# Decode through two attention and MLP layers: four loads of the key and value cache, whose ends are cut off and loaded in three pieces over 64, 63 and 1 or 64, 51 and 13 partitions

## The chip, the core and the metric

The kernel runs on one core of a Trainium2 chip. The metric is the device time of one execution in microseconds. Before the change it is 1355.34 us, the median of three runs (1352.47 to 1356.29). A difference of about 0.3% (4 us) is what three such runs can tell from no change.

## The reference

One token passes through attention and an MLP, and both once more with the same weights and the same cache:

```python
x = x + _A_ref(_layernorm(x, axis=-1), A_k_cache, A_v_cache, A_wq, A_wo)
x = x + _B_ref(_layernorm(x, axis=-1), B_w1, B_w2)
x = x + _A_ref(_layernorm(x, axis=-1), A_k_cache, A_v_cache, A_wq, A_wo)
x = x + _B_ref(_layernorm(x, axis=-1), B_w1, B_w2)
```

`_A_ref` makes a query of 128 numbers for each of 32 heads, scores it against 8192 cached keys, takes the softmax, and sums 8192 cached values by it; `wo` brings the 32 x 128 sums back to the 640 numbers of x. `_B_ref` is a product with w1 (640 x 1728), a ReLU, and a product with w2. Everything is float32. Keys and values of one head are 8 MB, those of all heads 256 MB, and each layer needs all of them: the cache is what is moved.

## The kernel before

The cache and part of w2 come through one buffer in SBUF, `ring`, 128 partitions wide and some 149 KB deep in each. The host has laid the cache out so that a load is a rectangle: each of the 128 partitions takes one contiguous run. A head has four pieces of keys (`K_ALL`) and four of values (`V_ALL`), each 8 KB per partition, 1 MB over all 128. `UNITS` says which pieces are loaded together. Heads 2 to 26 (`FULL`) are one unit of eight pieces, 64 KB per partition.

The list `todo` holds the loads in the order in which they will be issued (lines 119 to 155): layer 0 with the heads upwards, layer 1 with the heads downwards, since the last heads of layer 0 are partly kept. For the `FULL` heads, `turning` (lines 124 to 132) walks round the first 18 slots of 8 KB, and cuts a head in two where it passes the end. So head 9 of layer 0 is one load into slots 0 to 7, head 15 of layer 0 is a load of six pieces into slots 12 to 17 and one of two into slots 0 and 1; in layer 1, head 15 is one load into slots 8 to 15 and head 9 one into slots 2 to 9.

`pump` (lines 190 to 208) issues loads from `todo` as long as their place in the ring is free. All go through SP's queue, at line 204. `scores` (keys, line 448) and `values` (line 497) are the matmuls that read a piece; each ends with `release`, which frees the place and calls `pump`. Tile works out the waits: a load waits for the matmuls that read what it overwrites, and a matmul for the loads that wrote what it reads. A load that completes counts up one of eight semaphores, `DMAHW0` to `DMAHW7`, which SP's and ACT's loads use in turn; before a load takes one, its issuer waits until the load that had it eight issues ago is complete, unless a wait before has shown that already.

ACT's queue carries the weights: `wq` and `wo` by groups of four heads (`load_wq`, `load_wo`), w1 once, the rest of w2 once. Scores and values of a head alternate on PE with the softmax on ACT and DVE (`exponentials`, lines 461 to 482), and with side work for the projections. At the end of each layer stands the MLP, whose product with w2 is at line 419.

Of the kernel before, what the change touches and what calls it, by code (L numbers as in the profile page):

```python
# [18 lines left out]
SK = 8192  # L19
# [41 lines left out]
UNITS[31] = HALVES[:2] + LAST  # L61
DROPPED = {30: 2}
KEPT = 3800
MIX_AT = [12, 16, 20, 24]
AHEAD = 3

# [5 lines left out]
def kind_of(unit, t):  # L72

    return unit[0] if unit[0] != "kv" else "k" if t < len(K_ALL) else "v"


def wide(kind, piece):

    if kind == "w":
        return D // 8  # L80
    return 4 * piece[2] * (1 if kind == "k" else DH) // 8


def size(unit):
    return sum(wide(kind_of(unit, t), piece) for t, piece in enumerate(unit[1]))
# [9 lines left out]
W2_ALL = [("w2", i) for i in range(len(W2_RUNS))]  # L95
RING = KEPT + 4 * F_TILES * D // 8


@with_exitstack
def decode_kernel(ctx: ExitStack, tc: tile.TileContext, x, kv, wq, wo, w1, w2, w2_rest, out):  # L100
    nc = tc.nc
# [12 lines left out]
    ring = consts.tile([P, 8 * RING], F32, name="ring")  # L114
    order = [(h, i) for h in range(H) for i in range(len(UNITS[h]))]
    kept = [u for u in order if u[0] >= min(DROPPED) and u[1] >= DROPPED.get(u[0], 0)]
    assert sum(size(UNITS[h][i]) for h, i in kept) == KEPT
    beside = [(1, u) for u in order if u[0] == 30 and u not in kept]
# [37 lines left out]
    source = {}  # L156
    for us, dram in ((order, kv), (W2_ALL, w2)):
        o = 0
        for u in us:
            n = 8 * P * size(UNITS[u[0]][u[1]])  # L160
# [5 lines left out]
    def place(layer, u, n):  # L166

        step = 512 if n % 512 == 0 else 8
        if layer:
            low, high = 0, RING  # L170
        elif u[0] in range(FULL[0]):
            low, high = 0, 16 * SLOT
        elif u[0] == "w2":
            low, high = KEPT, RING
        else:
            low, high = (3072, KEPT) if n == KEPT - 3072 else (0, 3072)
        at, best = low, None
        for a, m in sorted(live.values()) + [(high, 0)]:
            a = min(a, high)
            for base in (0, KEPT):  # L180
                c = base + -(-max(at - base, 0) // step) * step
                if a - c >= n and (best is None or a - at < best[1]):
                    best = c, a - at
            at = max(at, a + m)
        return None if best is None else best[0]

    def is_free(at, n):
        return all(a >= at + n or a + m <= at for a, m in live.values())

    def pump():  # L190
        while todo:
            layer, u, first, last, at = todo[0]
            unit = UNITS[u[0]][u[1]]
            ns = [wide(kind_of(unit, t), piece) for t, piece in enumerate(unit[1])]
            n = sum(ns[first:last])
            if at is None:
                at = place(layer, u, n)
                if at is None:
                    return
            elif not is_free(at, n):  # L200
                return
            todo.pop(0)
            o = 8 * sum(ns[:first])
            nc.sync.dma_start(ring[:, 8 * at : 8 * (at + n)], source[u][:, o : o + 8 * n])
            for t in range(first, last):
                live[layer, u, t] = at, ns[t]
                at_of[layer, u, t] = ring, 8 * at
                at += ns[t]
# [13 lines left out]
    def release(L, u, t):  # L222
        if (L or u not in kept) and at_of[key(L, u, t)][0] is ring:
            del live[key(L, u, t)]
            pump()
# [22 lines left out]
    nc.sync.dma_start(xr, x)  # L248
    load_wq(0, nc.sync)
    pump()  # L250
    load_wo(0, nc.sync)

# [305 lines left out]
    def mixing():  # L558

        wc = mix[:, :D]  # L560
        s = work.tile([P, 1], F32, name="m_s")
        nc.vector.tensor_reduce(s, wc, AX.X, ALU.add)
        nc.vector.scalar_tensor_tensor(
            wc, s.to_broadcast([P, D]), -1.0 / D, wc, op0=ALU.mult, op1=ALU.add
        )
        yield "pe"
        pt = ps_m.tile([P, 512], F32, name="px")
        for c in range(4):
            nc.tensor.transpose(pt[:, c * P : (c + 1) * P], wc[:, c * DR : c * DR + P], ident)
        yield "dve"  # L570
        nc.scalar.copy(wct[:, :4].rearrange("p c d -> p (c d)"), pt)
        yield "pe"
        pt = ps_m.tile([P, 512], F32, name="px")
        for g in range(4):
            nc.tensor.matmul(
                pt[32 * g : 32 * g + 32, :P],
                wc[:, g * DR + P : (g + 1) * DR],
                ident,
                start=True,
                stop=True,  # L580
            )
        yield "dve"
        nc.scalar.copy(wct[:, 4], pt[:, :P])  # L583

    def mixing_quarter(g):

        pt = ps_m.tile([P, 512], F32, name="px")
        f, n = F_AT[g], F_ROWS[g]
        for c in range(NB):
            nc.tensor.matmul(  # L590
                pt[:, :n],
                wct[:, c],
                w1_t[:, c, f : f + n],
                start=(c == 0),
                stop=(c == NB - 1),
            )
            yield "pe" if c < NB - 1 else "dve"
        nc.scalar.copy(mix[:, f : f + n], pt[:, :n])
# [13 lines left out]
    def attention_and_mlp(L, xr, s):  # L612
# [68 lines left out]
        def due(h):  # L681
# [17 lines left out]
            if where == 11:  # L699
                slow.append([mixing(), "dve"])  # L700
            if where in MIX_AT:
                slow.append([mixing_quarter(MIX_AT.index(where)), "pe"])

# [264 lines left out]
```

## Time and profile before

| | before |
|---|---|
| median of 3 runs | 1355.34 us |
| the profiled execution, its own time | 1351.49 us |
| its span, first to last instruction | 1349.7 us |
| granted clock of TensorE, mean | 0.809 |
| busy: PE, PE's weight loads, DVE, ACT | 799.3, 270.4, 251.4, 59.2 us |
| bytes moved, mean pace | 575.17 MB, 426 GB/s |
| PE before line 448 (scores), idle for loads of the ring | 329.6 us |

The profile is of one execution, made by the hardware. Engines are PE (matmuls), PEld (its weight loads), DVE, ACT, POOL and SP; a q behind a name means the sequencer that waits and issues for it. L204 is line 204 of the kernel before. A DMA is issued by SP or ACT and carried out by 16 DMA engines that all loads share; the profile counts the packets that they moved, by queue (q1 is SP's, q10 ACT's, q8 and q14 fetch instructions), and the share of time in which the 16 were busy, but it doesn't name the engine of a packet. The busy time by window lists, for a stretch of time in us: its length, busy time and count of PE, PEld, DVE, ACT and POOL, the granted clock, the mean busy share of the 16 DMA engines, and GB/s. Shares a little over 1 come from packets that overlap. The chain lists what ended last at each step, in order of time: start, length, and the work.

### The profile page before, as it was taken

To read this page: it belongs to the slowest core of one execution; us is meant where nothing else is said; L and a number is where in the kernel's file an instruction comes from. 1 tells how busy PE (TensorE), PEld (TensorE's weight loads), DVE (VectorE), ACT (ScalarE), POOL (GpSimd) and SP (SyncE) were. 2 spreads that over 40 slices of the span, in tenths; PEclk is the share of its full clock that TensorE was granted. 3 is DMA by queue.
4 is the path that set the end of the run, shared out by engine and by line. 5 is a ranking of instruction groups with operands and counts; after the bars stand their busy time and mean duration, and the time that the engine had idled before them with its cause. 6 is when DMAs were issued, how large, how long until landed. Compare 5 with 4: busy or idle time off the path is not lost.

```text
span 1349.7 us, 13544 instructions
## 1 busy us (share of the span) xinstructions
PE 799.3 (59%) x6048; PEld 270.4 (20%) x6048; DVE 251.4 (19%) x794; ACT 59.2 (4%) x149; POOL 2.9 (0%) x10
## 2 busy tenths in 40 slices
PE   5455555554654655457787754555566554656658
PEld 2011111211211211122242211111121121212214
DVE  1111111221211211122122211122111211111212
ACT  0000000000000000000000000000000000000000
POOL 0000000000000000000000000000000000000000
PEclk8777677878978976788799777797778778777879
DMA  9999999999999999999999999999999999999997
GB/s 392 445 419 437 432 428 441 417 431 436 439 426 432 430 435 422 448 417 420 425 405 423 435 431 432 432 431 436 438 434 424 421 435 443 429 420 438 429 418 322
DMA packets 24977, 575.17 MB, mean 426 GB/s; under 512 B 2772, under 2 KB 2904, under 8 KB 5336
## 3 DMA queue, kind: packets, MB, share of 16 engines
q1 hardware_dynamic: 20312, 531.89, 91.8%
q10 hardware_dynamic: 4608, 42.44, 7.5%
q8 instruction: 47, 0.77, 0.2%
q14 instruction: 10, 0.08, 0.0%
HBM read 574.31 MB, written 0.00 MB: 426 GB/s over the span
## 4 chain that ended last, share of the span: by engine, by line
DMA 65%; PE 27%; DVE 5%; issue 1%; ACT 1%; ACTq 0%; SPq 0%; DVEq 0%
DMA ring<-in_kv 64%; PE ps L448 13%; PE outs L497 8%; DVE h_t L459 2%; PE px L387 1%; DVE pt L477 1%; PE pm L464 1%; ACT p L473 1%; DMA wo_t<-in_wo 1%; DVE p L516 1%; PE acc L419 1%; PE px L419 1%; PE acc L603 0%; PE px L590 0%; DVE pT L479 0%
## 5 line engine op out<-in xcount | busy, mean ns | idle before, releaser
L448 PE MATMUL ps<-ring,spread_q 128*32 128x512 f32 (+2 forms) x2072 | 331.0, 787 | 334.5 <-DMA ring<-in_kv 329.6
L497 PE MATMUL outs<-ring,pT 128*4 128x512 f32 (+1 forms) x2080 | 268.2, 658 | 27.7 <-DVE pT L479 17.4
L448 PEld LDWEIGHTS ps<-ring,spread_q 128*32 128x32 f32 x2072 | 76.9, 138 | 523.2 <-issue 298.4
L459 DVE TENSOR_REDUCE h_t<-ps 128x1 f32<-128x512 f32 x64 | 44.3, 692 | 640.3 <-PE ps L448 640.3
L473 ACT ACTIVATE p<-ps,h_t 128x512 f32<-128x512 f32 x64 | 44.0, 687 | 1226.4 <-DVE h_t L471 1226.4
L497 PEld LDWEIGHTS outs<-ring,pT 128*4 128x4 f32 x2080 | 52.5, 92 | 184.4 <-issue 156.9
L526 PE MATMUL pm<-ones,p 128*128 128x1 f32 x120 | 22.9, 260 | 94.8 <-DVE p L516 94.8
L512 DVE TENSOR_SCALAR p<-outs,ind 128x128 f32<-128x128 f32 x60 | 21.1, 351 | 248.2 <-PE outs L497 248.2
L516 DVE SCALAR_TENSOR_TENSOR p<-outs,ind,p 128x128 f32<-128x128 f32 x180 | 63.1, 351 | 6.4
L477 DVE STREAM_TRANSPOSE pt<-p 128x512 f32<-128x512 f32 x64 | 46.5, 727 | 57.9 <-ACT p L473 57.9
L464 PE MATMUL pm<-row_of,h_t 128*128 128x16 f32 x128 | 25.7, 276 | 49.9 <-DVE h_t L459 49.0
L526 PEld LDWEIGHTS pm<-ones,p 128*128 128x128 f32 x120 | 17.8, 188 | 151.5 <-DVE p L516 149.9
L464 PEld LDWEIGHTS pm<-row_of,h_t 128*128 128x128 f32 x128 | 19.4, 190 | 109.2 <-DVE h_t L459 107.3
L590 PE MATMUL px<-w_t,wct 128*128 128x448 f32 (+1 forms) x80 | 36.6, 573 | 1.1 <-ACT wct L583 1.1
L387 PE MATMUL px<-wq_t,ln_xc 128*32 128x256 f32 x280 | 32.9, 381 | 0.0
L486 PE MATMUL pm<-ind,h_t 128*128 128x1 f32 x128 | 23.4, 252 | 15.3 <-ACT p L473 15.3
L486 PEld LDWEIGHTS pm<-ind,h_t 128*128 128x128 f32 x128 | 23.2, 207 | 34.1 <-ACT p L473 26.6
L419 PE MATMUL acc<-wo_t,o_cols 128*32 128x160 f32 x496 | 22.7, 324 | 0.6 <-DVE o_cols L544 0.6
L527 DVE TENSOR_SCALAR o_cols<-pm,h_t 128x1 f32<-128x1 f32 x60 | 13.1, 218 | 30.6 <-PE pm L526 30.6
L387 PEld LDWEIGHTS px<-wq_t,ln_xc 128*32 128x32 f32 x280 | 15.2, 109 | 12.7 <-issue 1.2
L471 DVE TENSOR_REDUCE h_t<-pm 128x1 f32<-128x16 f32 x64 | 11.2, 175 | 32.4 <-PE pm L464 32.4
L419 PEld LDWEIGHTS acc<-wo_t,o_cols 128*32 128x32 f32 x496 | 15.8, 117 | 4.8 <-issue 2.5
(110 smaller groups left out, 201.2 us busy)
## 6 DMA issues: line engine op xcount, KB each, us to landing
ring<-in_kv SPq DMA_DIRECT2D x20, 4096.0 KB, 34.5
ring<-in_kv SPq DMA_DIRECT2D x38, 2048.0 KB, 29.3
ring<-in_kv SPq DMA_DIRECT2D x11, 6144.0 KB, 38.2
wq_t<-in_wq ACTq DMA_DIRECT2D x14, 1280.0 KB, 23.4
wo_t<-in_wo ACTq DMA_DIRECT2D x14, 1280.0 KB, 23.8
ring<-in_kv SPq DMA_DIRECT2D x15, 1024.0 KB, 16.7
ring<-in_w SPq DMA_DIRECT2D x4, 1280.0 KB, 26.8
w_t<-in_w ACTq DMA_DIRECT2D x1, 4320.0 KB, 47.7
```

The lines of the kernel that those rows point to most:

```text
L387: nc.tensor.matmul(pq[32 * j : 32 * j + 32, :n], xc[:, c : c + 1].to_broadcast([P, 32]), wq_t[g][:, c, j * n : (j + 1) * n], start=(c == 0 ...
L419: nc.tensor.matmul(acc[32 * g : 32 * g + 32, :DR], col.to_broadcast([col.shape[0], 32]), wt[:, g * DR : (g + 1) * DR], start=first, stop=last,
L448: nc.tensor.matmul(hd.ps[32 * g : 32 * g + 32, c : c + n], spread_q[:, 3 - r : 35 - r], tile_of[:, at + g * n : at + (g + 1) * n], start=f ...
L459: nc.vector.tensor_reduce(hd.nm, hd.ps, AX.X, ALU.max, negate=True)
L464: nc.tensor.matmul(pt[:, :16], hd.nm.to_broadcast([P, P]), row_of.rearrange("p g r -> p (g r)"), start=True, stop=True,)
L473: nc.scalar.activation(hd.p, hd.ps, AF.Exp, bias=hd.low, scale=1.0, accum_out=hd.l)
L477: nc.vector.transpose(pt, hd.p)
L486: nc.tensor.matmul(pt[:, :1], hd.l.to_broadcast([P, P]), ind[:, 4:5], start=True, stop=True)
L497: nc.tensor.matmul(hd.out[32 * g : 32 * g + 4, r : r + m].rearrange("p r d -> p (r d)"), hd.pT[:, 4 * i : 4 * i + 4], tile_of[:, v : v + m ...
L516: nc.vector.scalar_tensor_tensor(oc[:, r], hd.out[:, r], ind[:, r : r + 1], oc[:, r - 1], op0=ALU.mult, op1=ALU.add,)
L526: nc.tensor.matmul(pt[:, :1], oc[:, 3], ones, start=True, stop=True)
L590: nc.tensor.matmul(pt[:, :n], wct[:, c], w1_t[:, c, f : f + n], start=(c == 0), stop=(c == NB - 1),)
```

## The change

A new table, `SHARED`, names four heads by layer: a tail in units of 8 numbers per partition (SK // 32 is 8 KB, SK // 64 is 4 KB) and the rows of three pieces. In `pump`, a load that holds the last piece of such a head is issued without its last 8 or 4 KB per partition, and behind it the tail is issued in three loads: the first over partitions 0 to 63, the second over the next 63 or 51, the third over the last 1 or 13. Bytes, places in the ring and all that reads them stay as they are.

```diff
+SHARED = {
+    (0, 9): (SK // 32, [64, 63, 1]),
+    (0, 15): (SK // 64, [64, 51, 13]),
+    (1, 15): (SK // 32, [64, 63, 1]),
+    (1, 9): (SK // 64, [64, 51, 13]),
+}
...
-            nc.sync.dma_start(ring[:, 8 * at : 8 * (at + n)], source[u][:, o : o + 8 * n])
+            tail, groups = SHARED.get((layer, u[0]), (0, [])) if last == len(unit[1]) else (0, [])
+            nc.sync.dma_start(
+                ring[:, 8 * at : 8 * (at + n - tail)], source[u][:, o : o + 8 * (n - tail)]
+            )
+            p = 0
+            for rows in groups:
+                nc.sync.dma_start(
+                    ring[p : p + rows, 8 * (at + n - tail) : 8 * (at + n)],
+                    source[u][p : p + rows, o + 8 * (n - tail) : o + 8 * n],
+                )
+                p += rows
```

SP issues 154 loads and stores in place of 142; the order on the other engines is the same. On SP in layer 0, the loads of heads 7, 8, 9 and 10 stood like this (partitions x numbers of 4 bytes; `DMAHW` are the semaphores of the loads, `PE` that of the matmuls):

```order
L204 DMA ring<-in_kv 128x16384 [waits DMAHW5_49,PE_49]
L204 DMA ring<-in_kv 128x16384 [waits DMAHW7_49,PE_49]
L204 DMA ring<-in_kv 128x16384 [waits DMAHW1_49,DMAHW6_49,DMAHW0_49,PE_49]
L204 DMA ring<-in_kv 128x16384 [waits DMAHW3_49,PE_49]
L204 DMA ring<-in_kv 128x4096 [waits PE_49]
```

With the change the third of them, that of head 9, is followed by its tail:

```order
L211 DMA ring<-in_kv 128x16384 [waits DMAHW5_49,PE_49]
L211 DMA ring<-in_kv 128x16384 [waits DMAHW7_49,PE_49]
L211 DMA ring<-in_kv 128x14336 [waits DMAHW1_49,DMAHW6_49,DMAHW0_49,PE_49]
L216 DMA ring<-in_kv 64x2048 [waits PE_49]
L216 DMA ring<-in_kv 63x2048
L216 DMA ring<-in_kv 1x2048 [waits DMAHW2_49]
L211 DMA ring<-in_kv 128x16384 [waits DMAHW3_49,PE_49]
L211 DMA ring<-in_kv 128x4096 [waits DMAHW4_49,PE_49]
```

Three issues stand between the loads of heads 9 and 10, and the last of them has a wait of its own for an earlier load. The semaphores of all later loads move on by three. In layer 1 the same happens to heads 15 and 9; here is head 9 of layer 1 with the change, between heads 10 and 8:

```order
L211 DMA ring<-in_kv 128x12288 [waits DMAHW4_49,PE_49]
L211 DMA ring<-in_kv 128x4096 [waits DMAHW5_49,PE_49]
L211 DMA ring<-in_kv 128x15360 [waits DMAHW6_49,PE_49]
L216 DMA ring<-in_kv 64x1024 [waits PE_49]
L216 DMA ring<-in_kv 51x1024
L216 DMA ring<-in_kv 13x1024
L211 DMA ring<-in_kv 128x16384 [waits DMAHW7_49,PE_49]
```

The 4 KB tail has the rows 64, 51 and 13, and none of its three pieces waits for an earlier load, other than by the matmuls that free the place.

## The prediction

> **What bounds the kernel now.** I read the profile's page first: its span, the DMA rows of parts 2 and 3, and the shares of the chain that ended last.
>
> ```profile
> span 1349.7 us, 13544 instructions
> ...
> DMA  9999999999999999999999999999999999999997
> ...
> DMA packets 24977, 575.17 MB, mean 426 GB/s; under 512 B 2772, under 2 KB 2904, under 8 KB 5336
> ## 3 DMA queue, kind: packets, MB, share of 16 engines
> q1 hardware_dynamic: 20312, 531.89, 91.8%
> q10 hardware_dynamic: 4608, 42.44, 7.5%
> q8 instruction: 47, 0.77, 0.2%
> ...
> DMA 65%; PE 27%; DVE 5%; issue 1%; ACT 1%; ACTq 0%; SPq 0%; DVEq 0%
> ```
>
> The 16 DMA engines are 90% busy or more in 39 of 40 slices, and 65% of the chain is DMA. How full they are in the stages around the change is read from the busy time by window (the last two columns: mean busy share of the 16 engines, and GB/s). Heads 9 and 15 are loaded in the middle of each layer, so the first two windows are theirs; the next two are the seam between the layers.
>
> ```profile
> 100.00:300.00 200.00, 111.82 (x744) 33.87 (x744) 34.70 (x104) 7.44 (x19) 0.00 (x0) 0.75 1.00 431
> ...
> 950.00:1150.00 200.00, 106.88 (x768) 35.39 (x768) 35.13 (x107) 8.08 (x20) 0.00 (x0) 0.79 1.00 432
> ...
> 696.00:697.00 1.00, 1.00 (x12) 0.94 (x8) 0.46 (x3) 0.37 (x2) 0.00 (x0) 1.00 0.90 336
> 697.00:698.00 1.00, 0.88 (x24) 0.80 (x25) 0.53 (x5) 0.00 (x0) 0.00 (x0) 1.00 0.83 289
> ```
>
> In mid-layer all 16 engines work without a break, so an engine pace is 432/16 = 27 GB/s. At the seam they idle for (1 - 0.90) + (1 - 0.83) = 0.27 us on average. So the time is the work of the DMA engines plus little, and what counts is the engine that ends last. The end of the program shows that they don't end together.
>
> ```profile
> 1338.00:1339.00 1.00, 0.69 (x11) 0.37 (x14) 0.22 (x1) 0.00 (x0) 0.00 (x0) 1.00 1.04 430
> 1339.00:1340.00 1.00, 1.00 (x18) 0.53 (x10) 0.41 (x1) 0.00 (x0) 0.00 (x0) 1.00 0.71 292
> 1340.00:1341.00 1.00, 0.90 (x8) 0.76 (x8) 0.40 (x4) 0.37 (x2) 0.00 (x0) 1.00 0.57 241
> 1341.00:1342.00 1.00, 0.97 (x24) 0.70 (x24) 0.56 (x5) 0.00 (x0) 0.00 (x0) 1.00 0.48 200
> 1342.00:1343.00 1.00, 1.00 (x24) 0.94 (x26) 0.49 (x3) 0.00 (x0) 0.00 (x0) 1.00 0.53 206
> 1343.00:1344.00 1.00, 1.00 (x31) 0.49 (x26) 0.31 (x2) 0.00 (x0) 0.00 (x0) 1.00 0.39 164
> 1344.00:1345.00 1.00, 1.00 (x30) 0.72 (x22) 0.16 (x1) 0.00 (x0) 0.00 (x0) 1.00 0.11 46
> ```
>
> Nothing is queued behind these loads, so the share falls as engines run dry: from 16 at 1339 to about eight at 1341, and to none soon after 1344. About half of the engines are some 5 us late. The shares from 1339 on sum to 2.79 us: evenly dealt, all would end at 1341.8, some 2.5 us sooner than the last does. A likely cause of the lateness is instruction fetching, which takes engine time that the loads don't share evenly. One such fetch, alone in a window of 2 us (28.5 to 30.5):
>
> ```profile
> q8 instruction: 1, 0.02, 3.4%
> ```
>
> It took 3.4% of 16 x 2 us = 1.1 us, all of it one packet, so one engine's time. If the late half serves all 47, that is six each and 6.6 us by the last load, less what the early ones idle at the seam. No view names an engine, so which of the 16 are late is not shown.
>
> Last, the chain at the end. The last wait for a load that it shows ends at 1295.3; from there it is PE, DVE and ACT.
>
> ```profile
> 1266.60 28.68 DMA ring<-in_kv
> 1295.28 0.04 issue
> 1295.32 5.26 PE ps L448 x32
> ...
> 1344.75 1.81 PE px L419 x48
> ```
>
> That doesn't take the late engines off the path: the load at 1295.3 is itself complete only when its last engine is. Whatever delays the latest engine before 1295 delays the rest by as much.
>
> **The change part by part.** The bytes are the same. Per layer 1 MB (8 KB x 128 rows) of one head and 0.5 MB (4 KB x 128) of another are cut off and loaded in three pieces each.
>
> *How many engines take a narrow load.* ACT's queue tells what a wide one takes.
>
> ```profile
> wq_t<-in_wq ACTq DMA_DIRECT2D x14, 1280.0 KB, 23.4
> wo_t<-in_wo ACTq DMA_DIRECT2D x14, 1280.0 KB, 23.8
> w_t<-in_w ACTq DMA_DIRECT2D x1, 4320.0 KB, 47.7
> ...
> w_t<-in_w_rest ACTq DMA_DIRECT2D x1, 640.0 KB, 25.0
> mix<-in_wo ACTq DMA_DIRECT2D x2, 320.0 KB, 39.1
> ```
>
> These are 32 loads over 128 partitions, and q10 has 4608 packets: 144 each, 128 rows and 16 more, one closing packet for each engine. SP's queue has 141 such loads, 141 x 144 = 20304; the 8 that q1 has beyond are the store of the result over 4 partitions, four rows and four closings. So four rows went over four engines, not 16: rows are dealt in equal shares. I take it that the largest count up to 16 which divides the rows is used, and the same first engines each time: 64 rows over 16 (4 each), 63 over 9 (7 each), 51 over 3 (17 each), 13 over 13, 1 over 1. The Trainium skill, "DMA: Bandwidth & Descriptors", section "Why a DMA increments its semaphore by 16 and not by 1", states this rule, with the lowest-numbered engines; the count for the store agrees, the numbering no run shows.
>
> *What each engine then carries.* Before: 8 rows of 8 KB and 8 of 4 KB, 96 KB per layer. After, in KB: the first engine 32 + 56 + 8 + 16 + 68 + 4 = 184 (+88), the second and third 176 (+80), the fourth to ninth 32 + 56 + 16 + 4 = 108 (+12), the tenth to thirteenth 52 (-44), the last three 48 (-48). At 27 GB/s and over two layers that is +6.7, +6.1, +0.9, -3.3 and -3.6 us of an engine's work. Engines that never idle keep such a shift to the end.
>
> *What a load over half of the partitions runs at.* The trace has none. Lower bound: each engine keeps its 27 GB/s and nothing is lost. Upper bound: the pace belongs to the partitions written, so that 64 of them take half of the 432 GB/s and every load next to them waits; the pieces then cost their own time again, 1.57 MB / 432 GB/s = 3.6 us per layer, 7.3 us in all. A gain by narrowness itself has no row that would allow it, since each engine is full before. I take the upper end: the nearest rows, the two mid-layer windows, have all 128 partitions and all 16 engines at one pace, and nothing in them has room for 16 engines on 64 partitions to go on as before. The Trainium skill, "SBUF — State Buffer", section "Door 1: The DMA port swizzle", says so outright: partitions 0 to 63 reach 8 of 16 ports, and 1 MiB went at 196 GB/s over 64 partitions and 328 over 128. By that rule the pieces would add about 7 us, by the mid-layer rows alone anything from 0 to 7.3. No run here shows it yet.
>
> *Issues and waits.* Twelve more issues on SP; one takes 0.33 us (SP's timeline), and SP mostly waits (the waits of its queue: us, times, longest).
>
> ```profile
> 27.01 0.33 SPq L245 DMA_DIRECT2D wo_t<-in_wo  x1
> ```
>
> ```profile
> SPq L204 <- PE outs L497: 555.4, 72, 15.2
> SPq L204 <- DMA ring<-in_kv: 552.3, 74, 22.2
> ```
>
> That is 4 us beside 1108 us waited: nothing, while loads stay queued ahead (share 1.00); without that cover 1 us per head. Three of the pieces wait for the load eight issues back. In the queue behind such a wait stand the next heads' loads, and PE behind them; but by the order that load is of a head whose ring place has been overwritten, so it has landed: zero. The keys of a cut head wait for 7 MB or 7.5 MB and not 8: PE may start 1 to 2.4 us sooner, in a stage where engines and not releases set the pace: zero.
>
> *Sum.* Upper end 7.3 us for all engines. If the late ones are among the last seven, 7.3 - 3.3 = 4.0; if among the fourth to ninth, 7.3 + 0.9 = 8.2. I take the middle, +6.1: the profiled execution (1351.49, of which the span is 1349.7) becomes 1357.6. The median shown, 1355.34, lies 3.9 above that execution; the forecast goes on the median: 1361.4.
>
> **The rivals.**
>
> *Relief, not slower.* Narrow loads keep the engines' pace, and the late engines are among the last seven. Each loses up to 3.3 us of work; the end follows until others are last. The early ones have the 4.8 us between 1339.5 and 1344.3 and the seam for their +6.1, so the gain ends somewhere between 1 and 3.3, I say 2: 1353.3. For it: the even deal would gain 2.5 us by the windows, and there are about as many late engines as relieved ones. Against: it needs a particular set of engines and no loss at 64 partitions. It decides if the late engines are the tenth to sixteenth.
>
> *Load on the wrong engines.* No loss of pace, but a late engine is among the first three: +6.1 to 6.7, 1361.4 to 1362.0. For it: about half the engines are late, so three taken blindly hold one more often than not. Against: the deal may fit the late ones.
>
> *Both.* 7.3 + 6.1 or more: 1368.7.
>
> *Nothing.* The late ones are in the middle group at full pace (+0.9), or pieces are dealt evenly after all: 1355.3 to 1356.2.
>
> **How the numbers follow.** About 0.3%, 4.1 us, is what a measurement of this kernel can tell from no change (its three runs span 1352.47 to 1356.29). Chances: forecast 0.36 (its own range 1359.3 to 1363.5), relief 0.25, nothing 0.17, wrong engines 0.14, both 0.08. Slower: 0.36 + 0.14 + 0.08, less 0.05 for the low edge of the forecast: 0.53. Faster by over 4.1 us would need more than the largest relief: 0.06. The same: the other 0.41. The range 1352 to 1366 reaches from nearly all of the relief beyond the forecast's upper end, and leaves out "both" and some 0.06 of the relief.
>
> **What would show it.** Packets: each cut adds 128 rows, and closings 16 + 9 + 1 or 16 + 3 + 13; q1 should have 20312 + 4 x 128 + 2 x 26 + 2 x 32 = 20940. With the forecast, the windows where the four pieces land stay at a share near 1.00 but fall below 432 GB/s, by 1.2 to 4 us of time in all per layer. With relief, GB/s stays and the end falls from 16 engines to none in less than 5 us. With the wrong engines, the fall lasts longer, near 8 to 11 us. The forecast is wrong if GB/s doesn't fall at the pieces, and the sign is if the last load lands sooner.

## The result, and the profile after

The changed kernel takes 1374.01 us, the median of 4 runs (1373.09 to 1374.85), beside 1354.20 us (1352.47 to 1356.29) for the kernel before: ratio 1.0150, 95% interval 1.0137 to 1.0162. It is slower by 19.8 us, where +6.1 was forecast, and outside the range given. Its profiled execution spans 1371.8 us. The page first.

```profile
span 1371.8 us, 13570 instructions
...
DMA  9999999999999999999999999999999999999997
GB/s 392 434 435 429 438 431 355 429 431 435 390 429 438 433 422 424 436 426 422 425 412 425 433 440 422 431 438 429 436 386 392 432 425 405 418 416 442 426 417 293
DMA packets 25605, 575.17 MB, mean 419 GB/s; under 512 B 2888, under 2 KB 3020, under 8 KB 5708
...
q1 hardware_dynamic: 20940, 531.89, 91.6%
```

The engines are as full as before in every slice, and the bytes are the same, but four places of the GB/s row dip: 355, 390, 386 with 392, and 405. A slice is 34 us; by their times (225 to 245, 355 to 370, 1020 to 1035, 1155 to 1170 us) these are the loads of head 9 and head 15 of layer 0, then of 15 and 9 of layer 1. The busy time by window around them (last two columns: share of the 16 engines, GB/s), after:

```profile
215.00:245.00 30.00, 19.26 (x138) 5.82 (x138) 5.55 (x17) 1.55 (x4) 0.00 (x0) 0.72 1.00 346
345.00:380.00 35.00, 21.44 (x164) 7.25 (x156) 7.91 (x24) 2.09 (x5) 0.00 (x0) 0.89 1.01 391
1005.00:1045.00 40.00, 24.64 (x204) 9.11 (x208) 8.62 (x27) 1.55 (x4) 0.00 (x0) 0.83 0.98 353
1145.00:1180.00 35.00, 12.55 (x86) 3.97 (x82) 3.59 (x11) 1.28 (x3) 0.00 (x0) 0.71 1.01 384
```

The first and third of these windows in the kernel before:

```profile
215.00:245.00 30.00, 15.89 (x140) 5.54 (x140) 6.89 (x22) 1.56 (x4) 0.00 (x0) 0.89 0.99 428
...
1005.00:1045.00 40.00, 26.03 (x214) 8.84 (x210) 8.00 (x24) 1.56 (x4) 0.00 (x0) 0.88 0.99 426
```

What a window lost is its length x (1 - GB/s / 432): 30 x (1 - 346/432) = 6.0 us, then 3.3, 7.3 and 3.9, 20.5 us in all (0.5 before). So 20.0 of the 22.1 us between the two profiled spans lie at the four places, and at a share of 0.98 to 1.01: the engines hardly idle there, their packets take longer. At the worst spot, 1025 to 1030 us, the engines are still 91% busy, and yet fewer than half of the bytes come through (192 GB/s beside 432):

```profile
1020.00:1025.00 5.00, 3.78 (x34) 0.90 (x34) 1.42 (x6) 0.00 (x0) 0.00 (x0) 1.00 0.97 297
1025.00:1030.00 5.00, 0.38 (x2) 0.30 (x2) 0.57 (x2) 0.00 (x0) 0.00 (x0) 0.67 0.91 192
1030.00:1035.00 5.00, 4.17 (x28) 1.15 (x32) 0.00 (x0) 0.00 (x0) 0.00 (x0) 0.64 1.02 233
```

The end of the program, one window per us:

```profile
1360.00:1361.00 1.00, 0.69 (x8) 0.45 (x11) 0.22 (x1) 0.00 (x0) 0.00 (x0) 1.00 0.78 317
1361.00:1362.00 1.00, 1.00 (x17) 0.45 (x10) 0.28 (x1) 0.00 (x0) 0.00 (x0) 1.00 0.32 133
1362.00:1363.00 1.00, 1.00 (x8) 0.88 (x8) 0.46 (x3) 0.37 (x2) 0.00 (x0) 1.00 0.21 87
1363.00:1364.00 1.00, 0.88 (x25) 0.70 (x24) 0.53 (x5) 0.00 (x0) 0.00 (x0) 1.00 0.12 51
1364.00:1365.00 1.00, 1.00 (x24) 0.81 (x22) 0.49 (x4) 0.00 (x0) 0.00 (x0) 1.00 0.19 57
```

The fall lasts about 5 us, as before, but with fewer engines in it: from 1362 on a share of 0.12 to 0.21, two to three engines of 16, where before it was eight for 3 us.

### The profile page after: what moved, and what is told of

Read it like the earlier page. It is cut to its first block, busy times and chain, and to the rows that moved or that the text cites. A ratio compares the mean times of both kernels' runs of the same rounds, so it can differ in the third digit from the quotient of the medians.

```text
span 1371.8 us, 13570 instructions
## 1 busy us (share of the span) xinstructions
PE 794.5 (58%) x6048; PEld 271.0 (20%) x6048; DVE 251.4 (18%) x794; ACT 59.1 (4%) x149; POOL 2.9 (0%) x10
## 3 DMA queue, kind: packets, MB, share of 16 engines
q1 hardware_dynamic: 20940, 531.89, 91.6%
## 4 chain that ended last, share of the span: by engine, by line
DMA 64%; PE 28%; DVE 5%; issue 1%; ACT 1%; ACTq 0%; SPq 0%; DVEq 0%
DMA ring<-in_kv 63%; PE ps L464 14%; PE outs L513 8%; DVE h_t L475 2%; PE px L403 2%; DVE pt L493 1%; PE pm L480 1%; ACT p L489 1%; DMA wo_t<-in_wo 1%; DVE p L532 1%; PE px L435 1%; PE acc L435 1%; PE acc L619 1%; PE px L418 0%; DVE pT L495 0%
## 5 line engine op out<-in xcount | busy, mean ns | idle before, releaser
L464 PE MATMUL ps<-ring,spread_q 128*32 128x512 f32 (+2 forms) x2072 | 334.5, 795 | 361.7 <-DMA ring<-in_kv 356.8
L513 PE MATMUL outs<-ring,pT 128*4 128x512 f32 (+1 forms) x2080 | 256.1, 633 | 26.8 <-DVE pT L495 18.2
L502 PEld LDWEIGHTS pm<-ind,h_t 128*128 128x128 f32 x128 | 22.5, 202 | 34.1 <-ACT p L489 26.9
L487 DVE TENSOR_REDUCE h_t<-pm 128x1 f32<-128x16 f32 x64 | 11.2, 175 | 33.1 <-PE pm L480 33.1
```

Source lines behind the costliest of these rows:

```text
L464: nc.tensor.matmul(hd.ps[32 * g : 32 * g + 32, c : c + n], spread_q[:, 3 - r : 35 - r], tile_of[:, at + g * n : at + (g + 1) * n], start=f ...
L502: nc.tensor.matmul(pt[:, :1], hd.l.to_broadcast([P, P]), ind[:, 4:5], start=True, stop=True)
L513: nc.tensor.matmul(hd.out[32 * g : 32 * g + 4, r : r + m].rearrange("p r d -> p (r d)"), hd.pT[:, 4 * i : 4 * i + 4], tile_of[:, v : v + m ...
```

## The experiments

All keep the table's four heads and their 8 and 4 KB tails unless said otherwise; only the pieces differ. Each is compared with runs of the kernel before on the same chip. "Lost" is the sum over the four windows above by the same formula. It leaves out what an execution loses elsewhere: that of the two halves lost some 4 us more at the seam between the layers (700 to 800 us at 406 GB/s; 425 before and with the change).

| pieces of a tail | median, us | ratio (95% interval) | lost at the four places, us |
|---|---|---|---|
| 64, 63, 1 and 64, 51, 13 in order (the change) | 1374.01 | 1.0150 (1.0137 to 1.0162) | 20.5 |
| two halves | 1373.42 | 1.0149 (1.0128 to 1.0170) | 16.9 |
| even, odd | 1355.20 | 1.0009 (0.9999 to 1.0018) | 0.0 |
| the change's counts, even and odd | 1365.03 | 1.0090 (1.0063 to 1.0117) | 9.3 |
| 128 three times | 1354.04 | 1.0012 (1.0000 to 1.0024) | 0.9 |
| every eighth, 8 pieces | 1375.26 | 1.0166 (1.0140 to 1.0193) | 24.1 |
| middle 64 only | 1350.36 | 0.9982 (0.9971 to 0.9992) | 0.5 |
| lower 64 only | 1363.25 | 1.0068 (1.0051 to 1.0085) | 11.2 |
| 64 even, 60 and 4 odd | 1364.55 | 1.0082 (1.0061 to 1.0102) | 10.2 |
| 112 only | 1367.18 | 1.0090 (1.0065 to 1.0114) | 16.3 |
| 120 only | 1369.89 | 1.0120 (1.0101 to 1.0139) | 12.3 |
| every fourth, 8 pieces | 1364.71 | 1.0075 (1.0058 to 1.0093) | 12.3 |

**Narrowness, deal or issues.** The first four take the change apart. In place of a count, a piece is now a slice of partitions: first, end, step.

Two halves, dealt evenly:

```diff
-    (0, 9): (SK // 32, [64, 63, 1]),
+    (0, 9): (SK // 32, [(0, 64, 1), (64, 128, 1)]),
```

> The tails of the same four heads are cut off and loaded in two pieces, partitions 0 to 63 and 64 to 127: 64 rows each, which go over all 16 engines in equal shares, so the uneven deal is gone and the narrowness stays. Theory P (a load over one half of the partitions runs at about half pace and slows the loads beside it): most of the change's +19.8 us stays, at least the 7.3 us of the prediction's upper bound, and GB/s falls below 350 at the four places. Theory D (what costs is the deal: 63 rows over 9 engines, 51 over 3): within 3 us of the kernel before, GB/s near 432 at the four places. Theory W (issues and waits on SP's queue): two thirds or so of the cost, 8 added issues for 12, with GB/s near 432 and a share below 1.

Even and odd partitions:

```diff
+    (0, 9): (SK // 32, [(0, 128, 2), (1, 128, 2)]),
```

> The tails are loaded in two pieces of 64 rows, one over the even partitions and one over the odd ones: as many rows, engines, packets and issues as in the two halves, but each piece reaches both halves of the partitions. Theory P: no loss, within 3 us of the kernel before, GB/s at the four places near 432. Theory D: the same as the two halves, near zero. Theory W: the same as the two halves, and if those lose, this loses as much. If both the halves and this lose alike, it is the number of rows in a load, and not where they lie, that counts.

The change's counts over even and odd partitions:

```diff
+    (0, 9): (SK // 32, [(0, 128, 2), (1, 127, 2), (127, 128, 1)]),
+    (0, 15): (SK // 64, [(0, 128, 2), (1, 103, 2), (103, 128, 2)]),
```

> The change's own row counts, 64, 63 and 1 and 64, 51 and 13, so its own deal over engines, but the 64 are the even partitions and the rest the odd ones, so every piece reaches both halves. Theory P alone: within 3 us of the kernel before, or 1 to 3 us faster if the deal relieves late engines. Theory D: at least the prediction's +6.1 us, with a fall at the end that lasts 8 us or more; if D is the whole cause, near +19.8 us. Theory W: +19.8 us like the change, with the same 12 added issues.

Three cuts along the other axis:

```diff
+    (0, 9): (SK // 32, 3),
...
-            for rows in groups:
+            for i in range(groups):
+                a, b = (n - tail + 8 * (tail * j // (8 * groups)) for j in (i, i + 1))
                 nc.sync.dma_start(
-                    ring[p : p + rows, 8 * (at + n - tail) : 8 * (at + n)],
-                    source[u][p : p + rows, o + 8 * (n - tail) : o + 8 * n],
+                    ring[:, 8 * (at + a) : 8 * (at + b)], source[u][:, o + 8 * a : o + 8 * b]
                 )
```

> The tails are cut in three pieces along the other axis: each piece has all 128 partitions and a third of the 8 or 4 KB per partition. As many added issues and semaphores as the change, none of the narrowness and none of the uneven deal; smaller packets of 1.3 to 2.7 KB. Theory W: most of the +19.8 us. Theories P and D: within 3 us of the kernel before.

The first and third window, of the halves:

```profile
215.00:245.00 30.00, 18.89 (x146) 5.65 (x138) 5.55 (x18) 1.56 (x4) 0.00 (x0) 0.77 1.00 357
1005.00:1045.00 40.00, 25.24 (x202) 8.89 (x194) 7.99 (x24) 1.55 (x4) 0.00 (x0) 0.83 1.00 368
```

of even and odd:

```profile
215.00:245.00 30.00, 17.22 (x152) 5.67 (x143) 7.17 (x22) 1.56 (x4) 0.00 (x0) 0.88 1.00 426
1005.00:1045.00 40.00, 25.40 (x210) 8.77 (x202) 7.99 (x24) 1.56 (x4) 0.00 (x0) 0.88 1.00 430
```

and of the change's counts over even and odd:

```profile
215.00:245.00 30.00, 17.83 (x144) 5.77 (x140) 7.17 (x22) 1.56 (x4) 0.00 (x0) 0.83 1.01 394
1005.00:1045.00 40.00, 26.18 (x212) 9.46 (x216) 8.55 (x26) 1.56 (x4) 0.00 (x0) 0.83 1.00 395
```

The halves take as long as the change (ratio 1.0149 beside 1.0150; at the places 16.9 of the 20.5 us), with an even deal; pieces of as many rows over every second partition lose nothing. So the halves alone are enough for most of the cost, and neither the number of rows nor the added issues is. Twelve more issues with all 128 partitions cost 0.0 to 0.24%. But the deal costs too when the halves are avoided: 12 us, of which 9.3 stand at the places, with the share at 1.00 to 1.02. It isn't a longer fall at the end, as theory D wanted it: the share falls from 0.91 at 1352 us to nothing at 1356, some 4 us and not 8. The two don't add: 17 and 9 us at the places apart, 20.5 together. Theory P holds for the halves, though GB/s fell only to 357, 396, 368 and 397, where it asked for less than 350; D holds in the size for the deal and not in its mechanism.

**Which partitions.** Every eighth partition reaches both halves, so it tells the halves from the finer rule of the Trainium skill, "SBUF — State Buffer", section "Door 1: The DMA port swizzle": bits 4 to 2 and bit 6 of a partition's number choose one of 16 ports. The middle and the lower 64 are a pair of equal loads.

```diff
+    (0, 9): (SK // 32, [(0, 128, 8), (1, 128, 8), (2, 128, 8), (3, 128, 8), (4, 128, 8), (5, 128, 8), (6, 128, 8), (7, 128, 8)]),
```

> The tails are loaded in eight pieces of 16 rows, every eighth partition, beginning with 0, 1, 2 and 3 and then with 4, 5, 6 and 7. Each piece reaches both halves of the partitions, as the even and the odd ones did, which cost at most 3 us. Theory H (it is the lower or upper half of the partitions that has half the pace): no loss, within 3 us of the kernel before. Theory R (16 paths, each shared by the partitions that agree in bits 4 to 2 and in bit 6 of their number, as the Trainium skill has it; here the first four pieces reach the eight with bit 2 clear, the last four the other eight): a loss like that of the two halves, 10 to 20 us, and GB/s below 400 at the four places. Theory W' (28 more issues than before, in all, and waits on the load eight issues back): a loss with a share below 1.

```diff
+    (0, 9): (SK // 32, [(32, 96, 1)]),
```

> Only partitions 32 to 95 of each tail are loaded, in one piece of 64 rows; the other 64 rows of the tail aren't loaded, so 1.57 MB less is moved in all, worth 3.6 us. Theory R: the 64 rows reach all 16 paths, no loss: 3 to 4 us faster than before, GB/s near 432 at the four places. Theory H: they reach both halves, the same. Theory C (contiguous narrow loads cost, since their rows go to other engines than those of the wide loads beside them): slower than the kernel before by 3 us or more.

```diff
+    (0, 9): (SK // 32, [(0, 64, 1)]),
```

> The pair to the kernel that loads only the middle: only partitions 0 to 63 of each tail are loaded, the same 64 rows, packets, bytes and issues. Theories R and H: about half of what the two halves cost (10 us) less the 3.6 us: 5 to 8 us slower than before, and 9 us or more slower than the middle. Theory C: the same as the middle, within 3 us.

The third window of the middle 64:

```profile
1005.00:1045.00 40.00, 25.82 (x210) 8.48 (x199) 8.69 (x25) 1.56 (x4) 0.00 (x0) 0.87 0.99 426
```

and of the lower 64:

```profile
1005.00:1045.00 40.00, 26.80 (x214) 9.25 (x214) 8.00 (x24) 1.56 (x4) 0.00 (x0) 0.84 0.99 377
```

The two differ only in which 64 partitions they write (and in which rows of the source they read, at the same distance from each other), and by 1.0068/0.9982, 11.7 us. The middle is faster than before by 2.4 us (1.1 to 3.9 by the interval; its missing bytes are worth 3.6), and its windows show no loss: contiguous narrow loads are not slow as such. The lower 64 are slower by 9 us, a little more than the 5 to 8 expected. Every eighth partition loses more than the halves, so it isn't "lower and upper"; but its share falls below 0.95 at all four places, which the halves' did not, so something else is in it. Its third window:

```profile
1005.00:1045.00 40.00, 25.26 (x196) 8.66 (x197) 7.60 (x22) 1.56 (x4) 0.00 (x0) 0.83 0.88 353
```

Its control has as many pieces, but every fourth partition, in two cuts:

```diff
+    (0, 9): (SK // 32, [(0, 128, 4), (1, 128, 4), (2, 128, 4), (3, 128, 4)]),
...
+            for i in range(2 if groups else 0):
+                x, y = n - tail + i * tail // 2, n - tail + (i + 1) * tail // 2
```

> The control for every eighth partition: again eight pieces for each tail, but every fourth partition (32 rows, two for each engine, all 16 paths) in two cuts along the other axis, so as many issues and waits. If the loss of every eighth partition, 22 us, came of its paths: within 4 us of before. If of the eight pieces and the waits on loads eight issues back: 15 us or more, with a share below 0.95 at the places.

Two windows of it:

```profile
235.00:240.00 5.00, 3.41 (x20) 1.12 (x24) 1.27 (x5) 0.78 (x2) 0.00 (x0) 0.65 0.59 249
...
1025.00:1030.00 5.00, 2.39 (x18) 0.88 (x18) 1.62 (x5) 0.00 (x0) 0.00 (x0) 0.84 0.58 218
```

and the waits of its SP queue at the pieces' line:

```profile
SPq L217 <- DMA ring<-in_kv: 62.2, 8, 16.8
SPq L217 <- DMA wq_t<-in_wq: 30.6, 2, 18.9
```

It came out between the two expectations: 10 us lost, now mostly by idle engines. Eight pieces in a row use up the eight semaphores, which SP shares with ACT's loads; SP waits up to 18.9 us for the load eight issues back, and engines run dry meanwhile. So of the 22.5 us of every eighth partition some 10 are such waits and some 12 its paths (1.0166 against 1.0075), if the two add. The packet records of the trace, which give each row's time, bear the difference out. Between 200 and 260 us, 116 of the 128 rows of every eighth partition took over 5% longer than the shortest (307 ns for 8 KB; median 512), but only 39 of the 256 rows of every fourth (shortest 156 ns for 4 KB, median 159). With that, the rule of the bits agrees with these runs: pieces of 64 or 32 rows that reach the 16 ports alike keep their pace, and those over eight ports lose. One rival stays untested: each partition has its own rows of the source, so no run separates where a row is written from where it is read.

**How the price grows.** One head only (head 9 of layer 0), 56 of its 64 KB in halves:

```diff
-    (0, 9): (SK // 32, [64, 63, 1]),
...
+    (0, 9): (7 * SK // 32, [(0, 64, 1), (64, 128, 1)]),
```

> One head only (head 9 of layer 0), but 56 KB of its 64 KB per partition are loaded in the two halves, 3.67 MB each, so that a steady pace shows. Theory R or H at exactly half the pace: GB/s near 216 while they land, a loss of 7.34 MB / 432 GB/s = 17 us. Theory Q (the places of the change lost some 6 us per MB, which is a quarter of the pace, not half): GB/s near 120 and a loss of some 42 us. If the loss at the change's places lies in the beginning and end of the pieces and in their neighbours: 216 GB/s in the middle, and 17 us and a few more.

It took 1376.76 us, ratio 1.0172 (1.0148 to 1.0196). Its windows:

```profile
205.00:225.00 20.00, 13.02 (x110) 4.11 (x110) 3.59 (x11) 0.78 (x2) 0.00 (x0) 0.76 1.12 295
225.00:235.00 10.00, 0.73 (x4) 0.00 (x0) 0.00 (x0) 0.00 (x0) 0.00 (x0) 0.50 1.00 205
235.00:245.00 10.00, 0.00 (x0) 0.00 (x0) 0.00 (x0) 0.00 (x0) 0.00 (x0) 0.50 0.87 169
245.00:255.00 10.00, 0.00 (x0) 0.00 (x0) 0.00 (x0) 0.00 (x0) 0.00 (x0) 0.50 0.96 201
255.00:260.00 5.00, 3.03 (x16) 0.79 (x20) 0.00 (x0) 0.00 (x0) 0.00 (x0) 0.50 1.03 437
```

While the halves land, the pace is 205, 169 and 201 GB/s in the windows of 10 us, and 199 from 226 to 254 us, a little under half of 432. (The page of the Trainium skill named above has 196 GB/s for 1 MiB over partitions 0 to 63 and a limit of some 218 for larger loads; 199 lies between.) That is near the half pace and "17 us and a few more" of the third expectation; theory Q's 120 GB/s is out. By the windows 6.3 + 5.3 + 6.1 + 5.3 = 23.0 us are lost for 7.34 MB, 3.1 us per MB; the halves of the 8 KB tails lost 5.2 and 5.9 us for 1.05 MB, 5.3 us per MB, those of the 4 KB tails 2.9 and 2.8 us, as much per MB. So short pieces cost 1.7 times as much for their bytes as long ones. I first took the reason to be that the 16 engines are some us apart, so that narrow rows of early ones meet the wide rows of late ones, more so late in a layer. Two runs tried that: 8 KB halves in heads 3 and 25,

```diff
+    (0, 3): (SK // 32, [(0, 64, 1), (64, 128, 1)]),
+    (0, 25): (SK // 32, [(0, 64, 1), (64, 128, 1)]),
+    (1, 25): (SK // 32, [(0, 64, 1), (64, 128, 1)]),
+    (1, 3): (SK // 32, [(0, 64, 1), (64, 128, 1)]),
```

> 8 KB tails in two halves, as before in heads 9 and 15, but here in heads 3 and 25 of both layers: one place near the start and one near the end of each layer. Theory S (a place costs the bytes at about 195 GB/s instead of 432, 3 us for 1.05 MB, and beyond that an edge, since the engines are some us apart and those that are still at the wide load before share paths with those that are already at the narrow piece; they are further apart late in a layer): the early places lose 3 to 5 us each, the late ones 6 to 9. Theory E (the edge is the same everywhere, some 2.5 us): all four places lose 5 to 6 us, 22 us in all.

and the two halves again in heads 9 and 15, each tail in four cuts, with lower and upper pieces in turn:

```diff
+            for i in range(4 if groups else 0):
+                x, y = n - tail + i * tail // 4, n - tail + (i + 1) * tail // 4
+                for a, b, step in groups:
```

> The tails of heads 9 and 15 in halves, as in the first of these kernels, but each tail is first cut in four along the other axis: eight pieces, lower half, upper half, lower half and so on, of 2 or 1 KB per partition. Theory B (each step from a piece to one on the other half costs an edge of 2 us or so): 24 more steps, 40 us or more above the two halves' +20. Theory S (the edge comes once for each place): about the same +20, by 3. Theory M (engines that are us apart are at different halves at the same time when the pieces are short, so both halves' paths are in use): below +15. Should the share fall below 0.9 at the places, waits on the load eight issues back take part, and the run says less.

Early and late: 1377.55 us, ratio 1.0176 (1.0161 to 1.0191). The four places, early and late in layer 0, early and late in layer 1:

```profile
80.00:110.00 30.00, 19.50 (x146) 6.15 (x146) 6.42 (x22) 0.78 (x2) 0.00 (x0) 0.91 0.97 351
550.00:590.00 40.00, 18.32 (x146) 6.44 (x146) 6.57 (x21) 1.56 (x4) 0.00 (x0) 0.79 1.00 375
810.00:845.00 35.00, 14.78 (x100) 5.07 (x96) 5.94 (x18) 0.78 (x2) 0.00 (x0) 0.73 1.02 382
1270.00:1310.00 40.00, 23.38 (x196) 8.05 (x188) 7.91 (x24) 1.56 (x4) 0.00 (x0) 0.80 1.02 360
```

They lose 5.6, 5.3, 4.1 and 6.7 us: no growth in layer 0, and one of 2.6 us in layer 1, too little for theory S as it was put. Theory E, 22 us in all, comes nearer with 21.7. The alternating pieces took 1370.57 us, ratio 1.0127 (1.0112 to 1.0142): no step costs 2 us, so theory B falls. Theory M's +15 isn't reached. The +17 beside the halves' +20 is within the 3 us of theory S, and its interval meets that of the halves. The share falls to 0.42 at one place (1025 to 1030), so waits on the load eight back are part of it, and the run says no more.

The packet records tell where the price of short pieces lies. From each row's time, take off the usual time of a row of its size where nothing is slowed, sum the rest, and divide by the 16 engines. By this the 56 KB halves lost 18.6 us on their own rows (median 4401 ns for 2118) and 4.8 us on the rows of the other loads around them. The 8 KB halves of heads 9 and 15 lost 2.1 and 2.4 us on their own rows and 3.0 and 3.6 on the others, the 4 KB ones 0.8 and 0.7 on their own and 2.2 and 2.4 on the others. In heads 3 and 25 it was 1.2 to 2.6 us on their own rows and 2.0 to 4.9 on the others. So a piece's own loss goes roughly with its bytes, and that of its neighbours grows far less: by these sums it is the neighbours that make short pieces dear. Why their part has this size, and differs by place, stays open.

**Why the deal costs.** Three runs. 60 and 4 rows instead of 63 and 1:

```diff
+    (0, 9): (SK // 32, [(0, 128, 2), (1, 121, 2), (121, 128, 2)]),
```

> As in the kernel with the change's row counts on alternate partitions, but the odd partitions are loaded in pieces of 60 and 4 rows instead of 63 and 1 or 51 and 13: by the deal 15 engines get four rows of the 60, and four get one of the 4, so 15 engines carry about what they did and one carries half. Theory D (the loss of that kernel, 12 us, comes with the unevenness of the deal): within 3 us of the kernel before. Theory C' (any piece that isn't dealt over all 16 costs, by its neighbours on other rows): 8 to 12 us.

112 and 120 rows, the rest left out:

```diff
+    (0, 9): (SK // 32, [(0, 112, 1)]),
```

> Only partitions 0 to 111 of each tail are loaded, in one piece: 112 rows, seven for each of 16 engines; the last 16 rows aren't loaded, worth 0.9 us. Four of the 16 paths have half as many rows as the others, so some rows must go to another engine than the one whose path they lie on. Theory F (such rows collide with the loads beside them): 5 us or more slower than before, GB/s below 400 at the four places. Theory N (only loads over fewer than 16 engines, or over half the paths, cost): within 3 us of before.

```diff
+    (0, 9): (SK // 32, [(0, 120, 1)]),
```

> Only partitions 0 to 119 of each tail are loaded: 120 rows, eight for each of 15 engines by the deal; the last eight rows aren't loaded, worth 0.45 us. Nearly all paths are reached equally. Theory F: rows that are dealt in order over 15 engines lie on other paths than the wide loads' rows of the same engines: 5 us or more slower. Theory N: slower too, as 60 rows over 15 engines were. If it is neither, within 3 us of before, then it was the few partitions of the last small piece that cost in the kernel with 60 and 4 rows.

The third window of the 112 rows:

```profile
1005.00:1045.00 40.00, 24.32 (x194) 8.63 (x190) 8.00 (x24) 1.55 (x4) 0.00 (x0) 0.79 0.99 368
```

The near-even deal costs as much as the uneven one (1.0082 and 1.0090), so theory D's unevenness falls. 112 rows are shared by all 16 engines, seven each (q1 has 20824 packets, 20312 + 4 x (112 + 16)), so nothing is uneven; they lose 12 us all the same. Theory N falls with that, and F fits: what keeps its pace are loads that can be split over 16 engines so that each gets rows of one path only, as the wide loads can. The packet records show the slowing row by row. The time of one 8 KB row of the tails that land between 200 and 260 us (shortest, median, longest, ns):

```
even, odd             309  312  324
middle 64 only        309  313  324
64 even, 60 and 4 odd 309  380  558
the change's counts, even and odd
                      309  444  607
120 only              309  501  649
112 only              309  519  688
the change            309  546  726
lower 64 only         311  577  915
two halves            309  578  936
```

In the first two not one row in 192 is slowed, as if no two engines were ever on one path, though the engines are not in step: the 128 rows over even and odd partitions came over 7.4 us, and eight rows of 312 ns, an engine's share, take 2.5. In the others most rows are slowed, up to three times. Some rows of the wide loads beside them are too: a 64 KB row took 2418 to 2433 ns in that stretch before, and up to 4426 ns after (23 of 176 took over 5% longer than the shortest). Summed as above over the rows that begin near the four places (190 to 255, 330 to 385, 990 to 1050, 1130 to 1185 us), and divided by 16:

| pieces of a tail | rows of the tails, us | rows of all other loads there, us |
|---|---|---|
| the kernel before | none | 0.5 |
| the change | 5.8 | 14.2 |
| two halves | 6.0 | 11.2 |
| the change's counts, even and odd | 3.3 | 6.7 |
| 112 only | 5.0 | 10.8 |
| even, odd | 0.1 | 0.6 |
| middle 64 only | 0.0 | 0.8 |

So two thirds of what the change costs falls on other loads than its pieces. That each engine keeps to a path of its own in the wide loads is argued from this; no view names the engine of a packet.

## Why the prediction was wrong, by its own steps

**The bound** was read rightly: the DMA engines were and are full, and what delays them delays the end. **The deal's counts** were right: q1 has the 20940 packets that 16, 9 and 1 and 16, 3 and 13 engines give. That is a sum; no view shows which engine took a row.

**What a load over half of the partitions runs at** is the step that failed. It took for an upper bound that the pieces cost their own time again, 3.6 us per layer, 7.3 in all, and let that be the whole price, with the loads next to them only waiting as long. The direction was right: GB/s falls at the four places, at a full share. The size was not: 20.5 us by the windows, 6.5 us per MB where 2.3 was called the most. For the pieces' own rows the bound holds: they lost 5.8 us, and 6.0 as two even halves. But the rows of the other loads there were slowed as well, by 14.2 us (11.2 with the halves, 0.5 before), and the sum had no term for that. Where a narrow load is long the neighbours weigh less, and the bound nearly holds (3.1 us per MB in all, 2.5 by its own rows); for pieces of 1 MB and less it doesn't.

**What each engine then carries** treated the deal as a shift of bytes at 27 GB/s and nothing else. The shift may well be there: at the end two to three engines are last, the number that got +6.1 to 6.7 us. But the end takes no longer to fall than before. What the deal does cost stands at the places: the change's counts spread over all 128 partitions lose 12 us by themselves, where 64 and 64 rows lose none. By theory F the reason is rows on foreign paths; the row times fit it, and no view shows it engine by engine. No term of the sum was for this.

**Issues and waits** at zero was right for this change: share 1.00 at the places, and three wide pieces for one cost 0.12% (0.00 to 0.24%). The cover named was the right one: with eight pieces in a row it is gone, and 10 us are lost.

**The rivals.** Relief didn't happen, or is lost in the rest. "Both", 1368.7, came nearest, still 5.3 us short, and for the right reason in part, since narrowness and deal each cost. But it took them to add, and they overlap, and its price for the deal was that of late engines, not of slowed rows: that it came near is partly luck.

## What to carry to other kernels

When the DMA engines are full, ask of every narrow load which of the 16 paths its partitions reach and whether 16 engines can split it by them: 64 partitions from 32 to 95, or every second one, were as good as 128 here; the first 64 and the last 64, two pieces of 0.5 MB, cost with their neighbours some three times the time of their bytes. Don't shift bytes between engines by odd row counts: a load that doesn't split over 16 slows itself and its neighbours, which outweighed here any relief. A bound for a contended resource must include the work beside it, not only the piece itself.

## What the runs showed of the hardware that was not expected

- The rows of a load of 112 rows over 16 engines or of 120 over 15 are slowed (median of an 8 KB row 519 and 501 ns for 309), those of one of 64 rows over partitions 32 to 95 are not (313 ns).
- Rows of 64 KB in wide loads beside the pieces took up to 4426 ns for 2421, and the loads beside the pieces lost more time in all than the pieces: 14.2 us and 5.8.
- A full share of the DMA engines says nothing of their pace: 192 GB/s at a share of 0.91, beside 432 at 1.00.
- Eight small loads in a row are held up by the load eight issues back: SP waited up to 18.9 us, and the share fell to 0.58.
